# A second layer's first input: fetched through GpSimd's queue into a place of its own, split late by ScalarE

## The chip, the core and the metric

The kernel runs on one core of one Trainium2 chip. The metric is the device time of one execution in microseconds (us); lower is better. Three runs of the kernel before gave 1139.18, 1139.20 and 1141.53 us, median 1139.2 us. One core issues work to five engines: TensorE (PE in the profile; its weight loads are PEld), VectorE (DVE), ScalarE (ACT), GpSimd (POOL) and SyncE (SP). SP and POOL also issue DMAs, each in the order of its own queue.

## The reference

Three stages follow each other. A delta-rule attention (4 batches, 8 heads, 768 steps, 48 features per head) makes 3072 tokens of 384 features. Two feed-forward layers then work on these tokens:

```python
h = x @ w_in                                   # 3072 x 384 @ 384 x 2048
g = np.maximum(h, 0.0) + alpha * np.minimum(h, 0.0)
x = g @ w_out                                  # 3072 x 2048 @ 2048 x 384
h = np.maximum(x @ w2_in, 0.0)
out = h * h @ w2_out
```

## The kernel before, in words

**Precision.** Every operand of a large matmul is split into a high and a low part (`xh`, `xl`; `gh`, `gl`; `wh`, `wl`), and each product is three matmuls: high by high, high by low, low by high. The high part is a pass of ScalarE (a copy with a cast), the low part a subtraction on VectorE.

**Loops.** The first layer (layer 0) takes the tokens in 12 chunks of 256 (t = 0 to 11), the second (layer 1) in 6 chunks of 512. In each chunk, j runs over 16 slices of the 2048 hidden features. `emit_h` (line 623) makes h of slice j with 9 matmuls (L632), turns it into g and splits it: in layer 0 ScalarE's scaled copy (L110), VectorE's maximum (L639), ScalarE's `gh` (L644) and VectorE's `gl` (L645). `emit_acc` (line 648) multiplies g with the slice of the output weights in 9 matmuls (L664), three slices of j later in layer 0 and two later in layer 1, and adds them up in the accumulators in PSUM. After the last j, ScalarE copies the accumulators out (L673, tile `xf`), and SP stores them to `x2d` in DRAM (L675). The accumulators of the next chunk are the same banks, so its first L664 waits for L673 of the chunk before.

**Inputs of a chunk.** `load_x(n)` (line 551) fetches the input, `take_x(n)` (line 562) splits it. For n = 0 to 11 this is a chunk of the first layer. For n = 12 to 17 it is a chunk of the second layer, which consists of two halves of 256 tokens, each a load of 384 KB from `x2d` through SP (L560). One half goes into the tile `xf` of the pool `moe`, which has one buffer and which the first layer's inputs and outputs share; the other goes into a tile `xf` of the pool `w2`. `take_x` makes six ScalarE passes (L569) and six VectorE subtractions (L570): three blocks m of 128 features by two halves.

**Weights of the second layer.** `load_w1(j, i)` (line 723) fetches a raw block through GpSimd's queue into one of three buffers (L725) and unpacks it: a scaled copy on ScalarE (L110, `t<-raw`), four steps on VectorE (L589 to L592), an addition (L734), ScalarE's `wh` (L735), VectorE's `wl` (L736). That is 32 blocks; for each j the first (i = 0) holds the input weights, the second the output weights. The pool `w2` is opened when the attention's pools are closed, 20 steps before the end of the first layer, so this work runs beside the last two chunks of layer 0 and the first chunk of layer 1.

**What sets the order.** Work is emitted from a list of events by due time (`at`, `run_to`), in steps of one slice j of layer 0: chunk t has steps 16 t to 16 t + 15, and the second layer starts at step 192. The due time becomes a priority (`urgency`; earlier is more urgent). When the program is built, a planner simulates the engines and puts on each, whenever it is free, the most urgent instruction that is ready in the simulation. On the chip each engine then runs its instructions strictly in the order thus written down, whatever the real times are. `tc.issue_after(ins)` keeps instructions behind `ins` on the same engine. The due times around the change: `load_w1` 172 to 188.5; `load_x(12)` 187, `take_x(12)` 189; the last slices of layer 0 at 190 and 191; the first of layer 1 at 192.

**The tile `t` of pool `w`.** It has one buffer of 768 floats per partition. The attention writes its output there (line 523) before SP stores it to `x1d` (L528); after the last chunk of the attention nothing uses it.

Of the kernel before, what the change touches and what calls it, by code (L numbers as in the profile page):

```python
# [9 lines left out]
F32 = mybir.dt.float32  # L10
# [11 lines left out]
DM, DFF = 384, 2048  # L22
CH = 64
NCH = S // CH
NU = 2 * NCH
NG = 8
TOK = B * CH
KD = DM // 128
NF = DFF // 128
# [6 lines left out]
TT = -3  # L36
# [29 lines left out]
TB = 1  # L66
# [12 lines left out]
CHAIN = 4  # L79
EARLY = 3  # L80
INV = 15
WQ = 8
UR = 7
WN = 11
# [6 lines left out]
def kernel(ctx: ExitStack, tc: tile.TileContext, qT, ktok, vtok, beta, w1, w2, alpha, cmask, hmask, eye, ident, out):  # L91
    nc = tc.nc

    def pool(name, stack=ctx, **kw):
        return stack.enter_context(tc.tile_pool(name=name, bufs=1, **kw))

    e_stack, s_stack, w_stack = (ExitStack() for _ in range(3))
    const, moe, wpool = pool("const"), pool("moe"), pool("w")
# [5 lines left out]
    V, G, A = nc.vector, nc.gpsimd, nc.scalar  # L104

    def new(p, shape, dt, tag, bufs=1):
        return p.tile(shape, dt, tag=tag, name=tag, bufs=bufs)

    def scaled(out, in_, scale=1.0):
        A.activation(out=out, in_=in_, func=ACTF.Copy if isinstance(scale, float) else ACTF.Identity, scale=scale)  # L110
# [60 lines left out]
    x2d = [dram.tile([128, KD, 2, TOK], F32, tag=f"x2d{n}", name=f"x2d{n}") for n in range(NCH // 2)]  # L171
# [47 lines left out]
    def at(t, f, *a, ahead=0.0):  # L219
        heapq.heappush(events, (t, seq[0], f, a, ahead))  # L220
        seq[0] += 1
# [327 lines left out]
    xf = {}  # L549

    def load_x(n):

        if n < NCH:
            xf[n] = [new(moe, [128, KD, TOK], F32, "xf")]
            nc.sync.dma_start(out=xf[n][0][0:HD], in_=x1d[n][:, 0:KD])
            nc.sync.dma_start(out=xf[n][0][HD:128], in_=x1d[n][:, KD].rearrange("(m p) i -> p m i", m=KD))
        else:
            xf[n] = [new(moe, [128, KD, TOK], F32, "xf"), new(w2p[0], [128, KD, TOK], F32, "xf")]
            for h, t in enumerate(xf[n]):
                nc.sync.dma_start(out=t, in_=x2d[n - NCH][:, :, h])  # L560

    def take_x(n):
        src = xf.pop(n)
        p, k = (moe, XB) if n < NCH else (w2p[0], 1)
        xs[n] = [tuple(new(p, [128, len(src) * TOK], F32R, f"x{t}{m}", k) for t in "hl") for m in range(KD)]
        for m, (xh, xl) in enumerate(xs[n]):
            for h, t in enumerate(src):
                cols = slice(TOK * h, TOK * h + TOK)
                A.copy(out=xh[:, cols], in_=t[:, m])  # L569
                (G if m in TG and n < NCH else V).tensor_tensor(out=xl[:, cols], in0=t[:, m], in1=xh[:, cols].bitcast(F32), op=ALU.subtract)  # L570


# [21 lines left out]
    def load_w0(j):  # L594

        raw = new(wpool, [128, 4 * DM], F32, f"w{j}")
        if j < WQ:
            G.dma_start(out=raw.bitcast(I64), in_=w1[j])
# [19 lines left out]
            A.copy(out=wl[i], in_=ps[i])  # L618


    gt, acc = {}, {}

    def emit_h(layer, t, j):
        wh, wl = (t[0] for t in wt[layer, j])
        p, w = (w2p[0], 2 * TOK) if layer else (moe, TOK)
        ps = psum.tile([128, 512], F32, tag="h", name="h", bufs=2)[:, :w]
        n = 0
        for m in range(KD):
            sl = slice(m * 128, m * 128 + 128)
            xh, xl = xs[layer * NCH + t][m]  # L630
            for a, x in ((wh, xh), (wh, xl), (wl, xh)):
                nc.tensor.matmul(ps, lhsT=a[:, sl], rhs=x, start=(n == 0), stop=(n == 8))  # L632
                n += 1
        g = new(p, [128, w], F32, "r1", RB if layer else R1)
        if layer == 0:


            scaled(g, ps, sgn[:, j:j + 1])
            V.scalar_tensor_tensor(out=g, in0=ps, scalar=bet[:, j:j + 1], in1=g, op0=ALU.mult, op1=ALU.max)  # L639
        else:  # L640
            A.activation(out=g, in_=ps, func=ACTF.Relu)  # L641
            A.activation(out=g, in_=g, func=ACTF.Square)  # L642
        gh, gl = (new(p, [128, w], F32R, n, LAGB + 1 if layer else GB) for n in ("gh", "gl"))
        A.copy(out=gh, in_=g)  # L644
        (V if layer or j not in GP else G).tensor_tensor(out=gl, in0=g, in1=gh.bitcast(F32), op=ALU.subtract)  # L645
        gt[layer, t, j] = gh, gl

# [34 lines left out]
    for c in range(NCH):  # L682
# [17 lines left out]
        def scan(k=k, t=e0 + 9, n=IN):  # L700
            ops = inverse(k)
            for i, f in enumerate(ops):
                at(t + i * n / len(ops), f, ahead=(IA0, IA1)[k] if k < 2 else INV)
        if c % 2:
# [5 lines left out]
    for n in range(NCH + NCH // 2):  # L710
        t = 16 * n if n < NCH else 32 * n - 16 * NCH
        at(t - 5, load_x, n)
        at(t + TT, take_x, n)
    for j in range(NF):
        at(W0T + j, load_w0, j, ahead=AW)
    end = 16 * NCH
# [21 lines left out]
    w2p = []  # L738
# [7 lines left out]
    for layer, t, j in [(0, t, j) for t in range(NCH) for j in range(NF)] + [(1, t, j) for t in range(NCH // 2) for j in range(NF)]:  # L746
        step = 1 + layer
        now = 16 * NCH * layer + step * (16 * t + j)
        run_to(now)
        urgency(now - HURRY)  # L750
        emit_h(layer, t, j)
        run_to(now + 0.5 * step)
        pend.append((layer, t, j))
        urgency(now + 0.5 * step - HURRY)
        while len(pend) > (LAGB if layer else LAG):
            emit_acc(*pend.pop(0))
# [80 lines left out]
```

## Time and profile before

| | |
|---|---|
| median of three runs | 1139.2 us |
| profiled execution | 1140.61 us |
| its span | 1138.8 us |
| PE busy | 1054.2 us (93%) |
| DVE busy | 736.5 us (65%) |
| ACT busy | 728.6 us (64%) |
| mean granted clock of TensorE | 0.975 of full speed |

The span is what the trace covers; the execution has 1.8 us more around it, and it took 1.4 us more than the median of the three runs. A row of a timeline gives the start, the length, the engine, the line, the operation, what was written from what, and, in brackets, how long the engine had been idle before and what it had waited for. An engine whose queue is blocked by a wait stands still even if later work in its order is ready.

### The profile page before, as it was taken

How to read it: one execution, taken by the hardware profiler on the slowest of the kernel's cores; microseconds unless marked ns; L12 is line 12 of the kernel's file. 1: busy time of each engine (PE TensorE's matmuls, PEld its weight loads, DVE VectorE, ACT ScalarE, POOL GpSimd, SP SyncE). 2: the span in 40 equal slices, each digit the busy share in tenths (PEclk: the TensorE clock that was granted, in tenths of full speed). 3: DMA queues.
4: the chain of work that ended last, by engine and by line, in shares of the span. 5: the costliest groups of instructions: out<-in, count | busy, mean ns of one | idle time of the engine just before them, and what ended most of it. 6: DMA issues, size and time to landing. Idle time of an engine off the chain costs nothing.

```text
span 1138.8 us, 25230 instructions
## 1 busy us (share of the span) xinstructions
PE 1054.2 (93%) x9952; PEld 935.1 (82%) x9952; DVE 736.5 (65%) x1904; ACT 728.6 (64%) x1583; POOL 118.7 (10%) x206
## 2 busy tenths in 40 slices
PE   2766889899999979999999989999999999999997
PEld 2434579899999979999999989988888888888886
DVE  6998789699789869988986759888312121221211
ACT  7867678777767866885566546577645454454543
POOL 5111111111111111110110001011000000000000
PEclk9988899999999989999999989999999999999999
DMA  9585457545545464464353143343101000010000
GB/s 307 121 297 124 108 138 183 128 138 138 136 115 150 137 156 114 131 164 112 80 136 87 46 131 98 94 141 109 56 1 56 0 28 28 1 56 1 28 1 28
DMA packets 162886, 116.78 MB, mean 103 GB/s; under 512 B 122032, under 2 KB 143536, under 8 KB 162768
## 3 DMA queue, kind: packets, MB, share of 16 engines
q0 software_dynamic: 16320, 67.45, 19.3%
q1 hardware_dynamic: 146448, 47.73, 17.6%
q8 instruction: 78, 1.28, 0.5%
q14 instruction: 40, 0.33, 0.1%
HBM read 75.82 MB, written 39.32 MB: 101 GB/s over the span
## 4 chain that ended last, share of the span: by engine, by line
PE 73%; issue 8%; DMA 7%; DVE 6%; ACT 4%; SPq 1%; POOL 1%; POOLq 0%; ACTq 0%; DVEq 0%
PE h L632 32%; PE acc L664 31%; PE pa L133 3%; PE pa L123 3%; PE h L612 1%; DMA prob<-gscr 1%; DMA xf<-x2d 1%; PE h L613 1%; DMA xf<-x1d 1%; DMA al<-in_alpha_dram 1%; DMA gscr<-pf 1%; DMA vr<-in_vtok_dram 1%; ACT kbdE L110 1%; PE pe L351 0%; DVE w L590 0%
## 5 line engine op out<-in xcount | busy, mean ns | idle before, releaser
L632 PE MATMUL h<-xh,w 128*128 128x256 f32 (+1 forms) x1728 | 440.1, 325 | 4.7 <-DVE r L639 3.2
L664 PE MATMUL acc<-gh,w 128*128 128x256 f32 (+1 forms) x1728 | 431.8, 323 | 6.8 <-ACT xf L673 5.5
L632 PEld LDWEIGHTS h<-xh,w 128*128 128x128 f32 x1728 | 304.2, 192 | 29.8 <-DVE r L639 4.5
L645 DVE TENSOR_TENSOR gl<-r,gh 128x256 fp32r<-128x256 f32 (+1 forms) x288 | 145.4, 507 | 277.8 <-ACT gh L644 277.5
L664 PEld LDWEIGHTS acc<-gh,w 128*128 128x128 f32 x1728 | 299.1, 192 | 30.4 <-ACT xf L673 6.3
L632 PE MATMUL h<-xl,w 128*128 128x256 f32 (+1 forms) x864 | 278.5, 322 | 0.0
L664 PE MATMUL acc<-gl,w 128*128 128x256 f32 (+1 forms) x864 | 275.2, 322 | 3.6 <-DVE gl L645 3.4
L664 PEld LDWEIGHTS acc<-gl,w 128*128 128x128 f32 x864 | 165.2, 191 | 16.5 <-DVE gl L645 4.7
L632 PEld LDWEIGHTS h<-xl,w 128*128 128x128 f32 x864 | 166.2, 192 | 11.1
L644 ACT CAST gh<-r 128x256 fp32r<-128x256 f32 (+1 forms) x288 | 136.0, 476 | 52.9 <-DVE r L639 44.9
L641 ACT ACTIVATE r<-h 128x512 f32<-128x512 f32 x96 | 57.1, 596 | 148.0 <-PE h L632 141.2
L110 ACT ACTIVATE r<-h,sgn 128x256 f32<-128x256 f32 x192 | 89.9, 472 | 61.8 <-PE h L632 56.4
L639 DVE SCALAR_TENSOR_TENSOR r<-h,bet,r 128x256 f32<-128x256 f32 x192 | 90.9, 476 | 20.8 <-ACT r L110 19.9
L398 DVE TENSOR_TENSOR inv<-inv,col 128x252 f32<-128x252 f32 (+22 forms) x186 | 63.8, 343 | 1.7
L397 DVE TENSOR_TENSOR col<-prob,inv 128x252 f32<-128x252 f32 (+22 forms) x186 | 63.5, 341 | 1.5
L642 ACT ACTIVATE r<-r 128x512 f32<-128x512 f32 x96 | 60.7, 633 | 2.6
L123 PEld LDWEIGHTS <-kbd 96*128 96x128 f16 x1104 | 38.7, 99 | 7.7 <-issue 3.2
L612 PE MATMUL h<-w,idf 128*128 128x384 f32 x64 | 35.8, 648 | 7.3 <-ACT w L618 7.3
L133 PE MATMUL pa<-ph,ubd 128*128 128x64 f16 (+1 forms) x576 | 38.7, 194 | 0.9 <-ACT ubd L110 0.9
L569 ACT CAST xh<-xf 128x256 fp32r<-128x256 f32 x72 | 25.3, 403 | 20.0 <-DMA xf<-x2d 8.5
L570 DVE TENSOR_TENSOR xl<-xf,xh 128x256 fp32r<-128x256 f32 x72 | 26.6, 420 | 15.1 <-ACT xh L569 15.1
L133 PE MATMUL pa<-qh,sbd 96*128 96x64 f16 (+1 forms) x528 | 35.3, 194 | 0.0
(176 smaller groups left out, 1392.0 us busy)
## 6 DMA issues: line engine op xcount, KB each, us to landing
raw<-in_w_dram POOLq DMA_DIRECT2D x32, 384.0 KB, 3.4
kbd<-fscr POOLq DMA_DIRECT2D x22, 384.0 KB, 4.2
ktb<-kscr POOLq DMA_DIRECT2D x22, 384.0 KB, 3.6
kscr<-ktbE POOLq DMA_DIRECT2D x21, 384.0 KB, 3.4
fscr<-kbdE POOLq DMA_DIRECT2D x21, 384.0 KB, 3.4
w<-in_w_dram POOLq DMA_DIRECT2D x8, 768.0 KB, 9.2
w<-in_w_dram SPq DMA_DIRECT2D x8, 768.0 KB, 12.2
vr<-in_vtok_dram POOLq DMA_DIRECT2D x24, 192.0 KB, 4.1
```

Source lines behind the costliest of these rows:

```text
L110: A.activation(out=out, in_=in_, func=ACTF.Copy if isinstance(scale, float) else ACTF.Identity, scale=scale)
L123: nc.tensor.matmul(ps, lhsT=w[:, i], rhs=x[:, j], start=start and n == 0, stop=stop and n == 2)
L133: nc.tensor.matmul(ps[0:w.shape[1], g], lhsT=w, rhs=x[:, j, g], start=start and n == 0, stop=stop and n == 2)
L397: V.tensor_tensor(out=t, in0=row, in1=x[:, :, 0:m, j:j + 1].to_broadcast([128, 2, m, n]), op=ALU.mult)
L398: i = V.tensor_tensor(out=x[:, :, 0:m, j + 1:], in0=x[:, :, 0:m, j + 1:], in1=t, op=ALU.subtract)
L632: nc.tensor.matmul(ps, lhsT=a[:, sl], rhs=x, start=(n == 0), stop=(n == 8))
L639: V.scalar_tensor_tensor(out=g, in0=ps, scalar=bet[:, j:j + 1], in1=g, op0=ALU.mult, op1=ALU.max)
L641: A.activation(out=g, in_=ps, func=ACTF.Relu)
L642: A.activation(out=g, in_=g, func=ACTF.Square)
L644: A.copy(out=gh, in_=g)
L645: (V if layer or j not in GP else G).tensor_tensor(out=gl, in0=g, in1=gh.bitcast(F32), op=ALU.subtract)
L664: i = nc.tensor.matmul(acc[m], lhsT=a[:, sl], rhs=g, start=(j == 0 and n == 0 and (layer == 1 or m != 1)), stop=(j == NF - 1 and n == 2), ...
```

## The change

The second layer's first input (n = 12) is loaded by two DMAs of GpSimd's queue in place of SP's. Its first half goes into the tile `t` of pool `w` in place of the shared `xf`; the other half goes where it went. Its `take_x` is emitted at step 191.4 in place of 189, and its six ScalarE passes are kept behind `gh` of slice j = 14 (the fifteenth) of the last chunk of layer 0.

```diff
+XG = 1
...
         else:
-            xf[n] = [new(moe, [128, KD, TOK], F32, "xf"), new(w2p[0], [128, KD, TOK], F32, "xf")]
+            one = new(wpool, [128, 2 * DM], F32, "t", TB).rearrange("p (m i) -> p m i", m=KD) if n == NCH else new(moe, [128, KD, TOK], F32, "xf")
+            xf[n] = [one, new(w2p[0], [128, KD, TOK], F32, "xf")]
             for h, t in enumerate(xf[n]):
-                nc.sync.dma_start(out=t, in_=x2d[n - NCH][:, :, h])
+                (G if n == NCH and XG else nc.sync).dma_start(out=t, in_=x2d[n - NCH][:, :, h])
...
-                A.copy(out=xh[:, cols], in_=t[:, m])
+                with tc.issue_after(last[NF - 2]) if n == NCH else nullcontext():
+                    A.copy(out=xh[:, cols], in_=t[:, m])
...
-    gt, acc = {}, {}
+    gt, acc, last = {}, {}, {}
...
-        A.copy(out=gh, in_=g)
+        i = A.copy(out=gh, in_=g)
+        if (layer, t) == (0, NCH - 1):
+            last[j] = i.ins
...
-        at(t + TT, take_x, n)
+        at(t + (TT if n != NCH else -0.6), take_x, n)
```

## Rows read from the trace of the kernel before

**Rows 1.** The page: busy time by engine, and the last chain's share by line.

```profile
PE 1054.2 (93%) x9952; PEld 935.1 (82%) x9952; DVE 736.5 (65%) x1904; ACT 728.6 (64%) x1583; POOL 118.7 (10%) x206
...
PE h L632 32%; PE acc L664 31%; PE pa L133 3%; PE pa L123 3%; PE h L612 1%; DMA prob<-gscr 1%; DMA xf<-x2d 1%; PE h L613 1%; DMA xf<-x1d 1%; DMA al<-in_alpha_dram 1%; DMA gscr<-pf 1%; DMA vr<-in_vtok_dram 1%; ACT kbdE L110 1%; PE pe L351 0%; DVE w L590 0%
```

**Rows 2.** The chain followed back, 640 to 812 us: start, length, what.

```profile
662.26 6.96 DMA xf<-x2d
...
710.70 3.93 DMA xf<-x2d
...
737.99 0.24 PE acc L664 x2
...
740.29 1.91 PE acc L664 x16
```

**Rows 3.** Timeline of PE, around 667 and 716 us.

```profile
666.85 0.28 PE L664 MATMUL acc<-gh,w 128*128 128x256 f32 x1
671.02 0.58 PE L664 MATMUL acc<-gh,w 128*128 128x256 f32 x1 [3.89 <-ACT xf L673]
...
716.02 0.51 PE L664 MATMUL acc<-gh,w 128*128 128x256 f32 x2 [1.30 <-ACT gh L644]
717.04 0.39 PE L664 MATMUL acc<-gl,w 128*128 128x256 f32 x1 [0.51 <-DVE gl L645]
```

**Rows 4.** Windows: length, PE, PEld, DVE, ACT, POOL busy (count), PEclk, DMA share, GB/s.

```profile
671.02:676.73 5.71, 5.71 (x26) 5.71 (x27) 4.43 (x12) 1.93 (x5) 0.00 (x0) 0.50 0.44 142
717.04:721.27 4.23, 4.23 (x22) 4.23 (x23) 3.96 (x11) 2.20 (x6) 0.54 (x1) 0.60 0.00 2
722.00:738.00 16.00, 16.00 (x136) 16.00 (x135) 14.54 (x37) 9.07 (x22) 1.61 (x3) 1.00 0.31 94
745.00:785.00 40.00, 40.00 (x181) 33.20 (x181) 34.95 (x78) 29.21 (x57) 6.07 (x11) 1.00 0.43 129
```

**Rows 5.** Timeline of ACT, around 670 and 715 us.

```profile
669.32 1.02 ACT L569 CAST xh<-xf 128x256 fp32r<-128x256 f32 x3 [5.04 <-DMA xf<-x2d]
...
670.61 0.36 ACT L673 COPY xf<-acc 128x256 f32<-128x256 f32 x1
670.86 0.56 ACT L110 ACTIVATE t<-raw 128x384 f32<-128x384 f32 x1
...
714.65 1.02 ACT L569 CAST xh<-xf 128x256 fp32r<-128x256 f32 x3 [3.49 <-DMA xf<-x2d]
```

**Rows 6.** SP's queue, 640 to 765 us, and landing of x1d's stores.

```profile
656.39 5.33 SPq L528 DMA_DIRECT2D x1d<-t  x2
...
710.70 0.57 SPq L560 DMA_DIRECT2D xf<-x2d  x1
...
x1d<-t SPq DMA_DIRECT2D x2, 192.0 KB, 2.7
```

**Rows 7.** Line L725 (raw blocks, GpSimd's queue), 655 to 676 us.

```profile
L725 POOL DMA_DIRECT2D raw<-in_w_dram x3: 536/538/540, 661.7 to 662.7; - x3
...
DMA to landing us min/median/max: 4.7/5.4/6.5
```

**Rows 8.** Timeline of DVE: the two groups of three subtractions.

```profile
669.75 1.10 DVE L570 TENSOR_TENSOR xl<-xf,xh 128x256 fp32r<-128x256 f32 x3 [5.02 <-ACT xh L569]
...
715.09 1.10 DVE L570 TENSOR_TENSOR xl<-xf,xh 128x256 fp32r<-128x256 f32 x3 [2.91 <-ACT xh L569]
```

**Rows 9.** Timeline of ACT: `gh` of the last chunk's fifteenth slice.

```profile
736.38 0.41 ACT L644 CAST gh<-r 128x256 fp32r<-128x256 f32 x1 [0.59 <-DVE r L639]
```

**Rows 10.** Timelines of ACT and DVE: splitting the second layer's second input.

```profile
801.21 2.07 ACT L569 CAST xh<-xf 128x256 fp32r<-128x256 f32 x6 [0.81 <-PE h L632]
...
801.65 2.12 DVE L570 TENSOR_TENSOR xl<-xf,xh 128x256 fp32r<-128x256 f32 x6 [0.66 <-ACT xh L569]
```

**Rows 11.** The second layer's slice j = 15: `wh` on ACT, first matmul on PE.

```profile
796.86 0.55 ACT L735 CAST w<-raw 128x384 fp32r<-128x384 f32 x1 [0.38 <-DVE raw L734]
...
798.97 0.39 PE L632 MATMUL h<-xh,w 128*128 128x512 f32 x1
```

## The prediction

> **What bounds the kernel now.** I read the page first: TensorE is busy for 93% of the span, and the chain that ended last is mostly its matmuls L632 and L664 [rows 1]. That chain's lines also name a transfer, xf<-x2d, 1% of the span. Following the chain through 640 to 812 us shows where: twice, for 6.96 and 3.93 us, the end of the kernel hangs on a load of a second-layer input [rows 2], in the middle of the first layer. From 722 us on TensorE has no idle time in the windows read [rows 4], so a microsecond it saves before can reach the end, if nothing else comes late.
>
> What do the two loads hold up? ScalarE's timeline says it: it stands 5.04 us in front of three passes L569 and later 3.49 us in front of the other three [rows 5]. The order is fixed, so all behind them waits. At 669 us that is L673, the copy that frees an accumulator: TensorE stops for 3.89 us until L673 of 670.61 [rows 3, 5]. At 714 us it is a gh: TensorE stops for 1.30 us, then for 0.51 us on its gl [rows 3]. None of these six passes is needed before layer 1 begins at 738 us.
>
> **The two stalls, in TensorE's time.** Undisturbed, 136 matmuls take 16.00 us, 0.118 us each, at a granted clock of 1.00 [rows 4]. After the first stop 26 matmuls took 5.71 us at 0.50 (the 1.2 GHz level), which is 5.71 - 26 x 0.118 = 2.6 us too many; after the second 22 took 4.23 us, 1.6 us too many [rows 4]. So the first stall costs 3.89 + 2.6 = 6.5 us, the second 1.30 + 0.51 + 1.6 = 3.4 us, together 9.9 us.
>
> **What the change removes.** The passes go behind the fifteenth slice's gh, which begins at 736.38 us [rows 9], so neither stop can be caused by them. On the TensorE side that is worth up to 9.9 us. SP's queue loses both loads; the second of them could only be issued at 710.70 us, because it used the shared tile [rows 6]. The second half's tile is now freed late, so SP's load of the second layer's second input into that tile moves behind the passes, to about 740 us; its reader is at 801.21 us [rows 10], so that costs nothing, and it would cost only if it landed some 60 us late.
>
> **What it adds.** (a) Two DMA issues on GpSimd, about 0.54 us each as the raw blocks have [rows 7], on an engine busy for 1.61 of 16 us [rows 4]; the data is wanted 70 us later. Nothing is lost if they stand behind the three raw loads that start at 661.7 us. If they stand ahead, those wait until the last x1d store has left tile t: its issue ends at 661.7 us (656.39 + 5.33), it lands about 2.7 us after its issue [rows 6]. They then also share the transfer with two more blocks. The raw landings of 4.7, 5.4 and 6.5 us after issues 0.5 us apart [rows 7] put one block at about 1.4 us. That is 2.3 + 2 x 1.4 = 5 us later at worst, nothing or a small gain at best; I take nothing, since the raw loads are due long before (172 against 187).
>
> In the rows the first raw block landed 4.7 us after its issue with SP's load beside it [rows 7]. The Trainium skill, DMA: Bandwidth & Descriptors, section "Queues, rings and completion order", says that a DMA engine takes turns between queues and works through one queue in order. By that the x loads, moved into the raw blocks' queue, hold back none that stands ahead of them, and the first block could even land some 0.5 us sooner; every block behind them waits for both. The sum stays as it is; no run here shows it yet.
>
> (b) Six passes and six subtractions directly before layer 1's first h. At the next chunk boundary the same twelve took 801.21 to 803.77 us, 2.6 us [rows 10]. From the end of gh at 736.8 us that is 739.4 us. Before, 18 matmuls of L664 stood after the last h of layer 0 [rows 2]; 2.1 us of them can stand ahead of the waiting h, from 738.0 to 740.1 us. So the loss is 0 at one end. At the other end no L664 covers and VectorE, busy for 14.54 of 16 us [rows 4], is slow: 739.4 - 738.0 plus about 1 us, some 2.4 us. I take 0.5 us.
>
> **What is late next: the weights of layer 1.** The stream of blocks runs mostly on VectorE, beside the end of layer 0 and the first chunk of layer 1, and its last slice comes just in time: wh of j = 15 is ready at 796.86 + 0.55 = 797.41 us, its first matmul starts at 798.97 us [rows 11]: 1.6 us of slack. TensorE can gain 9.9 us only if this stream gains 8.3. Its start: the first t<-raw ran at 670.86 us, behind the stopped passes [rows 5], while its block had landed at 661.7 + 4.7 = 666.4 us [rows 7]: 4.4 us to gain. In the second stop VectorE stood for 2.91 us [rows 8], which it gains. The first three subtractions (1.0 us) ran before the stream and now run inside it: 1.0 us lost; the other three were inside already. Sum 4.4 + 2.9 - 1.0 = 6.3, with the slack 7.9 us.
>
> **Sum.** The smaller of 9.9 - 0.5 and 7.9 is 7.9 us. TensorE then waits some 1.5 us before j = 15, close to the 1.81 us after which the clock fell and cost 1.6 us. I take half, 0.8: the gain is 7.1 us, and 1140.6 becomes 1133.5 us for an execution like the profiled one. Against the median (1.4 us less) it is 1132.1 us.
>
> **Rivals.**
> Free: weights come in time after all and all 9.9 us count, less 0 to 0.8: 1129.3 to 1130.1 us. For it: without the stops VectorE may fill its gaps better (5 of 40 us in 745 to 785 [rows 4]). Against: the 1.6 us of slack. Chance 0.14.
>
> The stream does not start earlier: the x loads ahead of the raw blocks (5 us, above), or ScalarE waiting for a raw block in front of L673, which leaves part of the first stop. Then the weights gain 0 + 2.9 - 1.0 + 1.6 = 3.5 us: 1135.7 us. In favour: the blocks landed between 666.4 and 669.2 us, while L673 is wanted at 667. Against: the planner had put L673 before t<-raw [rows 5]. Chance 0.18.
>
> Nothing measurable: that rival, and the boundary takes 2.4 us more: gain 1.1, 1138.1 us. A change without its effect belongs here too: the planner orders the rest anew, and ScalarE stands at another wait for as long. Chance 0.07.
>
> Slower: the six subtractions (2.1 us) have a later due time than all the weight work, and VectorE's idle share is only 1.46 of 16 us [rows 4]. If they get that share alone, they take 2.1 / 0.091 = 23 us. The 18 matmuls cover 2.1 us, TensorE stops 21 us and loses 2.6 us more at the low clock: 23.6 - 9.9 = 13.7 us slower, 1152.9 us. It decides from some 9.6 us of stop on (9.6 + 2.6 - 9.9 = 2.3). Against: a stopped TensorE leaves VectorE without layer 0's work, so the share grows. Chance 0.06.
>
> **Numbers.** My forecast, 1132.1 us, has the remaining 0.55, from 1130.5 us (no clock loss) to 1134.5 us (boundary at its upper end). 0.2%, about what a measurement of this kernel can tell from no change, is 2.3 us. Faster by more: 0.55 + 0.14 + 0.18 = 0.87; within: 0.07; slower: 0.06. The range takes in the free case and the late stream with about 0.5 us: 1129.2 to 1136.2 us; outside lie the last two cases and the edges.
>
> **What would show it.** Right: no ACT wait on xf<-x2d before 736 us, no PE gap on L673 near 667, a granted clock of 1.00 from 664 to 722, t<-raw near 666.5, layer 1's first 512-column matmul near 728 to 729, its six passes just before, and a PE gap of 1 to 2 us before j = 15, near 790 us, with its wh some 6 us earlier than the 797.41 us of now. Wrong: a gap at the boundary over 3 us; a raw landing after 669 us; a PE gap at L673 that stays; or no gap at all near 790, which makes the free case true.

## The result, and the profile after

The changed kernel took 1132.13 us (median of 13 runs, 1129.48 to 1136.72), the kernel before on the same chips 1143.12 us (13 runs, 1139.18 to 1148.42). The ratio is 0.9906, 95% interval 0.9884 to 0.9928: faster by 10.7 us, between 8.2 and 13.3 (the medians alone differ by 11.0 us). The forecast time of 1132.1 us agrees better than its reasons deserve. It set a gain of 7.1 us off against 1139.2 us, the median of three runs, and both the gain and the kernel before came out larger.

The profiled execution after the change took 1134.28 us, its span 1132.5 us. Lines have moved by a few: L569 is L572 (passes), L570 is L573 (subtractions), L632 is L635, L664 is L669, L673 is L678, L725 is L730, L735 is L740, L639 is L642.

The page, against [rows 1]: the transfer xf<-x2d is gone from the last chain.

```profile
PE 1053.3 (93%) x9952; PEld 933.1 (82%) x9952; DVE 736.5 (65%) x1904; ACT 727.8 (64%) x1583; POOL 121.0 (11%) x208
...
PE h L635 30%; PE acc L669 30%; PE pa L134 3%; PE pa L124 2%; ACT kbdE L111 1%; DMA prob<-gscr 1%; PE h L615 1%; DMA gscr<-pf 1%; PE h L616 1%; DMA vr<-in_vtok_dram 1%; DMA al<-in_alpha_dram 1%; ACT kf L111 1%; ACT r L111 0%; DVE gl L650 0%; ACT w L621 0%
```

The timeline of TensorE after, against [rows 3]. Of the 3.89 us in front of the accumulators 0.73 are left; the stops of 1.30 and 0.51 us have no successor. One chunk later TensorE waits 0.35 us for the same kind of copy. Layer 1 begins at 732.20 us.

```profile
671.54 0.38 PE L669 MATMUL acc<-gh,w 128*128 128x256 f32 x1 [0.73 <-ACT xf L678]
...
703.31 0.39 PE L669 MATMUL acc<-gh,w 128*128 128x256 f32 x1 [0.35 <-ACT xf L678]
...
732.20 0.40 PE L635 MATMUL h<-xh,w 128*128 128x512 f32 x1
...
792.28 0.39 PE L635 MATMUL h<-xh,w 128*128 128x512 f32 x1
```

Windows after, against [rows 4] (length, PE, PEld, DVE, ACT, POOL, PEclk, DMA share, GB/s): the clock stays at 1.00 right behind the 0.73 us, and from 714 us on TensorE has no listed idle time.

```profile
671.54:676.00 4.46, 4.46 (x37) 4.46 (x38) 4.46 (x13) 2.88 (x7) 0.00 (x0) 1.00 0.64 222
...
714.00:732.00 18.00, 18.00 (x153) 18.00 (x152) 17.38 (x46) 11.34 (x29) 2.56 (x5) 1.00 0.36 103
...
740.00:800.00 60.00, 60.00 (x270) 49.78 (x269) 51.17 (x113) 41.99 (x83) 8.00 (x14) 1.00 0.38 114
```

ScalarE and GpSimd after, against [rows 5, 7, 9]. ScalarE still stands in front of the accumulator copy L678, 2.35 us, now for the first raw weight block. The six passes run without a wait from 730.51 us. GpSimd issues the two x loads behind three raw blocks.

```profile
670.32 0.54 ACT L111 ACTIVATE t<-raw 128x384 f32<-128x384 f32 x1 [2.35 <-DMA raw<-in_w_dram]
...
671.13 0.36 ACT L678 COPY xf<-acc 128x256 f32<-128x256 f32 x1
...
730.51 0.41 ACT L572 CAST xh<-t 128x256 fp32r<-128x256 f32 x1
...
789.96 0.53 ACT L740 CAST w<-raw 128x384 fp32r<-128x384 f32 x1
```

```profile
665.38 1.60 POOL L730 DMA_DIRECT2D raw<-in_w_dram  x3 [33.99 <-PE acc L669]
666.97 0.77 POOL L562 DMA_DIRECT2D xf<-x2d  x1
668.08 0.76 POOL L562 DMA_DIRECT2D t<-x2d  x1 [0.34 <-issue]
```

**A measure that leaves the noise out.** The two programs have the same instructions in the same order up to the place of the first pass on each engine; only SP's first load is missing. Yet the first raw block of layer 1's weights was issued at 661.7 us before ([rows 7]) and at 665.4 us after. What the change does lies behind this issue. So I use the *stretch*, from this issue to the end of the span: 1138.8 - 661.68 = 477.1 us before, 1132.5 - 665.38 = 467.1 us after. The change takes 10.0 us out of it in this pair of profiles, each of which is one execution.

### The profile page after: what moved, and what is told of

Read it like the earlier page. It is cut to its first block, busy times and chain, and to the rows that moved or that the text cites. A ratio compares the mean times of both kernels' runs of the same rounds, so it can differ in the third digit from the quotient of the medians.

```text
span 1132.5 us, 25229 instructions
## 1 busy us (share of the span) xinstructions
PE 1053.3 (93%) x9952; PEld 933.1 (82%) x9952; DVE 736.5 (65%) x1904; ACT 727.8 (64%) x1583; POOL 121.0 (11%) x208
## 4 chain that ended last, share of the span: by engine, by line
PE 69%; issue 10%; DMA 7%; ACT 7%; DVE 6%; POOL 1%; SPq 1%; POOLq 0%; DVEq 0%; ACTq 0%
PE h L635 30%; PE acc L669 30%; PE pa L134 3%; PE pa L124 2%; ACT kbdE L111 1%; DMA prob<-gscr 1%; PE h L615 1%; DMA gscr<-pf 1%; PE h L616 1%; DMA vr<-in_vtok_dram 1%; DMA al<-in_alpha_dram 1%; ACT kf L111 1%; ACT r L111 0%; DVE gl L650 0%; ACT w L621 0%
## 5 line engine op out<-in xcount | busy, mean ns | idle before, releaser
L635 PE MATMUL h<-xh,w 128*128 128x256 f32 (+1 forms) x1728 | 438.4, 324 | 4.2 <-DVE r L642 2.6
L669 PE MATMUL acc<-gh,w 128*128 128x256 f32 (+1 forms) x1728 | 429.7, 321 | 2.1 <-ACT xf L678 2.0
L635 PEld LDWEIGHTS h<-xh,w 128*128 128x128 f32 x1728 | 302.9, 192 | 29.2 <-DVE r L642 3.5
L669 PEld LDWEIGHTS acc<-gh,w 128*128 128x128 f32 x1728 | 297.6, 190 | 25.7 <-ACT xf L678 2.8
L669 PE MATMUL acc<-gl,w 128*128 128x256 f32 (+1 forms) x864 | 274.5, 322 | 4.6 <-DVE gl L650 4.5
L635 PE MATMUL h<-xl,w 128*128 128x256 f32 (+1 forms) x864 | 277.6, 322 | 0.0
L669 PEld LDWEIGHTS acc<-gl,w 128*128 128x128 f32 x864 | 164.4, 190 | 17.3 <-DVE gl L650 5.6
L635 PEld LDWEIGHTS h<-xl,w 128*128 128x128 f32 x864 | 165.6, 192 | 11.1
L642 DVE SCALAR_TENSOR_TENSOR r<-h,bet,r 128x256 f32<-128x256 f32 x192 | 90.9, 476 | 16.4 <-ACT r L111 15.1
L134 PEld LDWEIGHTS <-ubd 128*128 128x128 f16 (+1 forms) x576 | 31.1, 100 | 2.1 <-ACT ubd L111 1.2
L124 PE MATMUL pa<-qh,kbd 96*128 96x64 f16 x576 | 30.3, 196 | 2.7 <-DVE uh L120 1.0
```

Of the source, the lines that this page charges most:

```text
L124: nc.tensor.matmul(ps, lhsT=w[:, i], rhs=x[:, j], start=start and n == 0, stop=stop and n == 2)
L134: nc.tensor.matmul(ps[0:w.shape[1], g], lhsT=w, rhs=x[:, j, g], start=start and n == 0, stop=stop and n == 2)
L669: i = nc.tensor.matmul(acc[m], lhsT=a[:, sl], rhs=g, start=(j == 0 and n == 0 and (layer == 1 or m != 1)), stop=(j == NF - 1 and n == 2), ...
```

## The experiments

All numbers of the traces in one table (us). "First t<-raw" and "wh 15" (ScalarE's pass for slice 15's input weights of layer 1) are counted from the first raw block's issue; "VectorE idle" is VectorE's idle time from the first unpacking step to wh 15. Each row is one profile. A "ratio" below is that of timed runs to the kernel before: e1, e3 and e6 were timed in 10 to 12 executions, the other experiments rest on their one profiled execution.

| kernel | span | raw issue | stretch | first t<-raw | wh 15 | VectorE idle |
|---|---|---|---|---|---|---|
| before | 1138.8 | 661.68 | 477.1 | 9.2 | 135.2 | 15.0 |
| before, again (e11) | 1142.0 | 663.74 | 478.3 | 9.8 | 136.9 | 16.3 |
| change | 1132.5 | 665.38 | 467.1 | 4.9 | 124.6 | 8.2 |
| change, again (e10) | 1138.7 | 671.30 | 467.4 | 5.0 | 124.6 | 7.6 |
| e1 passes late only | 1134.6 | 667.68 | 466.9 | 5.0 | 123.5 | 7.7 |
| e2 loads only | 1131.3 | 663.23 | 468.1 | 4.5 | 125.1 | 8.7 |
| e3 loads on SP | 1135.5 | 668.42 | 467.1 | 4.7 | 123.5 | 8.1 |
| e4 first stop removed | 1137.8 | 667.14 | 470.7 | 5.0 | 129.4 | 12.5 |
| e5 second stop removed | 1134.8 | 661.47 | 473.3 | 9.4 | 132.2 | 12.6 |
| e6 copy first | 1132.5 | 665.36 | 467.1 | 4.7 | 123.8 | 7.8 |
| e7 16 more copies | 1139.3 | 665.08 | 474.2 | 4.9 | 135.6 | 12.8 |
| e8 32 more copies | 1144.3 | 668.77 | 475.5 | 4.7 | 136.4 | 10.7 |
| e9 passes behind slice 15 | 1139.3 | 669.95 | 469.4 | 5.0 | 125.1 | 8.4 |

### How well the stretch repeats (e10, e11)

Both kernels unchanged, profiled once more.

> The changed kernel once more, for how well the stretch repeats: 467.1 us within 0.3 us, while the time ahead of the first raw block's issue (665.4 us in the profile shown) may differ by some us. If the stretch is off by over 1 us, the differences of 1 us between the other kernels say nothing.

> The kernel before once more: stretch 477.1 us within 0.5 us (it holds two stops on transfers), both stops at the same matmuls and as long within 0.5 us.

The change repeats within 0.3 us. The kernel before comes out 1.1 us longer, more than the half microsecond expected, because its stops are longer by 0.6 and 0.8 us: here TensorE's timeline of e11, where [rows 3] had 3.89 and 1.30 us.

```profile
673.70 0.58 PE L664 MATMUL acc<-gh,w 128*128 128x256 f32 x1 [4.52 <-ACT xf L673]
...
719.31 0.50 PE L664 MATMUL acc<-gh,w 128*128 128x256 f32 x2 [2.12 <-ACT gh L644]
```

From this one repeat of each I take a profile of the changed kernel as good to some 0.3 us and one of the kernel before to about 1 us; the second pair gives 478.3 - 467.4 = 10.9 us. The two pairs bracket the 10.7 us of the timed runs. Some 0.4 us of either difference lies behind the last store and has nothing to do with the stops; e3 shows it.

### Passes late, loads as before (e1)

```diff
-                A.copy(out=xh[:, cols], in_=t[:, m])
+                with tc.issue_after(last[NF - 2]) if n == NCH else nullcontext():
+                    A.copy(out=xh[:, cols], in_=t[:, m])
...
-        at(t + TT, take_x, n)
+        at(t + (TT if n != NCH else -0.6), take_x, n)
```

> Loads as before (SP's queue, one half in the shared tile), only the six ScalarE passes late. Measure: the stretch from the first raw block's issue to the end of the span, 477.1 us before and 467.1 us after the change; the work ahead of it is the same list of instructions. Theory A (the place of the passes in ScalarE's queue is all): both stops go, 466.2 to 467.6 us, ratio to before 0.990 to 0.993. Rival B (the loads' own place and queue bring the gain): at least 3.4 us of it is missing, 470 us or more.

Stretch 466.9 us, ratio 0.9919 (0.9893 to 0.9945): the late passes alone bring all of it. TensorE (length, PE, PEclk, DMA share, GB/s) has no gap at all in the first 20 us:

```profile
667.68:687.68 20.00, 20.00 (x169) 1.00 0.59 177
```

Rival B falls as far as it says that the loads are needed.

### Loads as in the change, passes early (e2)

```diff
-                with tc.issue_after(last[NF - 2]) if n == NCH else nullcontext():
+                with nullcontext():
...
-        at(t + (TT if n != NCH else -0.6), take_x, n)
+        at(t + TT, take_x, n)
```

> Loads as in the change (GpSimd's queue, own place), passes due as early as before and free to stand anywhere. Theory A: ScalarE comes to the passes near 672 us while the loads, issued at 667 and 668 us behind three raw blocks, land some 4 to 6 us later; it stands 1 to 3 us, TensorE stops behind it for up to 2 us: stretch 468 to 471 us. Rival B: the loads alone bring the whole gain, 467 us, with no wait of ScalarE on them.

Stretch 468.1 us: 9.0 of the 10.0 us come from the loads alone too. ScalarE does wait for one of them, 1.30 us, and TensorE stops for 0.28 and 0.89 us, without a lower clock. First ScalarE, then TensorE of e2, last its window behind the 0.89 us, with the columns of [rows 4]:

```profile
671.32 1.02 ACT L572 CAST xh<-xf 128x256 fp32r<-128x256 f32 x3 [1.30 <-DMA xf<-x2d]
673.38 1.00 ACT L572 CAST xh<-t 128x256 fp32r<-128x256 f32 x3
```

```profile
668.95 0.38 PE L669 MATMUL acc<-gh,w 128*128 128x256 f32 x1 [0.28 <-ACT xf L678]
...
677.89 0.39 PE L635 MATMUL h<-xh,w 128*128 128x256 f32 x1 [0.89 <-DVE r L642]
```

```profile
677.89:681.89 4.00, 4.00 (x33) 4.00 (x34) 3.41 (x9) 1.59 (x4) 0.55 (x1) 1.00 0.81 250
```

In e2 the planner puts the passes a few places later in ScalarE's order, behind the accumulator copy and one more slice, and the second half no longer waits for the shared tile. The two halves of the change are two cures for one thing; together they bring hardly more than either. The figures that theory A gave for this run came out, at their lower edge; as the statement that the late passes are what counts it is too narrow.

### The loads on SP's queue (e3)

```diff
-XG = 1
+XG = 0
```

> The change with its two loads on SP's queue instead of GpSimd's. Theory A: the queue is worth nothing, stretch 466.2 to 467.6 us. Rival C (GpSimd's queue spares something, because SP's loads stand beside the raw blocks or SP's queue is blocked by them): the first raw blocks land over 1 us later than after the change and the stretch is 1 us longer or more, over 468 us.

Stretch 467.1 us, ratio 0.9923 (0.9897 to 0.9949), the first t<-raw 4.7 us after the raw issue against 4.9: for the time of the whole the queue is worth nothing here. The prediction had weighed the Trainium skill's DMA: Bandwidth & Descriptors, "Queues, rings and completion order", for a first block some 0.5 us sooner behind a shared queue, a figure for which it gave no working. In the chain after the change the first block took 4.71 us from its issue, the same 4.7 us as with SP's load beside it [rows 7], so the runs do not show that half microsecond; that the loads stood behind the blocks and held none of the first three back agrees. The slowest of the first three blocks did land sooner, 5.6 us after its issue against 7.0 in e3, so that part of rival C is right; the stretch was no shorter for it. The first block's transfer after the change, and the landings of the first three blocks after the change and in e3:

```profile
665.38 4.71 DMA raw<-in_w_dram
...
DMA to landing us min/median/max: 4.7/5.2/5.6
...
DMA to landing us min/median/max: 4.5/5.3/7.0
```

Nothing in sum is not nothing in each part. In e3 the planner left the accumulator copy ahead of the first t<-raw, the gap of 0.73 us is absent, and ScalarE's last copy of the kernel begins 0.4 us sooner, at 463.1 us of the stretch against 463.5. But from the issue of the last store to the end of the span e3 takes 3.3 us and the change 3.0. The last store of the change, then of e3:

```profile
1129.49 0.33 SPq L674 DMA_DIRECT2D out_dram<-r  x1
...
1132.15 0.33 SPq L674 DMA_DIRECT2D out_dram<-r  x1
```

At the end SyncE waits for its transfers one by one, and the order of these waits differs: after the last store has landed, seven more of them (some 0.06 us each) follow in e3 and one after the change. The profiles divide by the queue: 3.3 us in the kernel before, its repeat, e1, e3, e4 and e5, and 3.0 us in the change, its repeat, e2 and e6 to e9.

### One stop at a time (e4, e5)

Kernel before with a `last` as in the change; in e4 only the half in pool `w2` (h = 1), in e5 only the half in the shared tile (h = 0) is kept late:

```diff
-                A.copy(out=xh[:, cols], in_=t[:, m])
+                with tc.issue_after(last[NF - 4]) if n == NCH and h == 1 else nullcontext():
+                    A.copy(out=xh[:, cols], in_=t[:, m])
```

> Kernel before, only the three passes of the half in pool w2 (the first stop, 5.04 us) kept behind gh of slice j = 12 of the last chunk; loads and the other three passes as before. Stretch from the first raw block's issue to the end: 477.1 us before. Theory A (the stops add up, 6.5 and 3.4 us, and the stream of weights follows TensorE): 470.2 to 471.0 us, the second stop as before. Rival D (the stream of weights gains only its earlier start, 4.4 us, less three subtractions, 1.0 us, and has 1.6 us of slack, as the prediction's sum had it): TensorE stops before slice 15 of layer 1, 472.1 us or more.

> Kernel before, only the three passes of the half in the shared tile (the second stop, 3.49 us) kept behind gh of slice j = 12 of the last chunk. Theory A: the first stop as before (about 3.9 us and the low clock after it), the second gone, 473.4 to 474.1 us. Rival E (the second stop hides behind the first: with it gone TensorE meets the stream of weights sooner): 475 us or more, with a gap before a slice of layer 1.

Stretches 470.7 and 473.3 us: 6.5 and 3.8 us gained, where the prediction had 6.5 and 3.4 (against the longer second profile of the kernel before, 1.1 us more each). TensorE's timeline of e4, then of e5, shows that in each the other stop stays:

```profile
716.70 0.50 PE L668 MATMUL acc<-gh,w 128*128 128x256 f32 x2 [0.96 <-ACT gh L646]
717.73 0.39 PE L668 MATMUL acc<-gl,w 128*128 128x256 f32 x1 [0.53 <-DVE gl L649]
```

```profile
670.98 0.58 PE L668 MATMUL acc<-gh,w 128*128 128x256 f32 x1 [4.07 <-ACT xf L677]
```

Together 10.3 us, so the stops add up, as far as one profile each can tell. Rival D's gap before slice 15 in e4 did not come.

### The last small gap (e6)

```diff
-        scaled(t, high.bitcast(F32), 2.0 ** -112)
+        with tc.issue_after(last["o"]) if (j, i) == (0, 0) else nullcontext():
+            scaled(t, high.bitcast(F32), 2.0 ** -112)
```

where `last["o"]` is chunk 9's second accumulator copy (m = 1), the one TensorE waited for.

> The change, and the first unpacking pass of layer 1's weights (t<-raw) kept behind the accumulator copy that TensorE waited 0.73 us for at 671 us. Theory A: that gap goes and nothing else moves, stretch 466.2 to 466.6 us against 467.1. Rival: the stream of weights starts no earlier and the gap turns into another wait, 467 us or more.

The gap of 0.73 us is gone, and the stretch is 467.1 us as before it; ratio 0.9926 (0.9902 to 0.9951). The rival is right. The 0.7 us reappear in pieces too short for the timeline's brackets, just before the next chunk of layer 0: in 12 us there TensorE began 90 matmuls in e6, and 97 in the same 12 us after the change, at the same clock. Seven matmuls at 0.118 us are 0.8 us. What held them up in e6 was not tried. The window of e6, then of the change, with the columns of [rows 4]:

```profile
693.36:705.36 12.00, 11.83 (x90) 10.90 (x89) 12.00 (x32) 8.62 (x23) 1.11 (x2) 1.00 0.32 100
...
693.38:705.38 12.00, 11.65 (x97) 11.40 (x96) 11.83 (x31) 8.73 (x24) 1.49 (x3) 1.00 0.27 87
```

e1 and e3 have no gap of 0.73 us either and end within 0.2 us of the change; they are ahead of it at the last copy, by 0.6 and 0.4 us, and lose most of that in the longer end described at e3.

### More work in the stream of weights (e7, e8)

```diff
         V.tensor_tensor(out=f, in0=high.bitcast(F32), in1=f, op=ALU.add)
+        if 2 * j + i < 16:
+            V.tensor_copy(out=f, in_=f)
```

(e8: 32 in place of 16.) The copies are needless work and change no value.

> The change, and one needless VectorE copy of 128x384 in each of the first 16 of the 32 weight blocks of layer 1, about 0.3 us each, some 5 us in all. Rival D (the stream is VectorE's alone and has 1.8 us of slack before slice 15): TensorE stops for 3 us, stretch 470 us or more against 467.1. Theory A (the stream has idle VectorE time ahead of it, 9 of 60 us from 740 to 800, and catches up): 467.0 to 468.0 us, no gap of 1 us before a slice of layer 1.

> The same needless copy in all 32 blocks, some 10 us in all, more than VectorE's idle time in the stretch. Rival D: 475 us or more. Theory A: part is taken from idle time, part not: 468 to 472 us, with TensorE's gaps in the last slices of layer 1's first chunk.

Stretches 474.2 and 475.5 us. In e7 VectorE's busy time from the first unpacking step to wh 15 rose from 110.9 to 117.4 us, 6.5 us, and the stretch by 7.1 us: the stream did not catch up, as rival D said. The time is lost at the last slices of layer 1's first chunk, by the pattern this case began with: ScalarE stands for a transfer, a gh behind it is late, TensorE stops. The transfer itself was issued late, after GpSimd had stood 4.30 us for VectorE. GpSimd, ScalarE, then TensorE of e7:

```profile
791.20 0.54 POOL L730 DMA_DIRECT2D raw<-in_w_dram  x1 [4.30 <-DVE raw L592]
...
794.84 0.56 ACT L111 ACTIVATE t<-raw 128x384 f32<-128x384 f32 x1 [1.99 <-DMA raw<-in_w_dram]
...
798.29 0.62 ACT L647 CAST gh<-r 128x512 fp32r<-128x512 f32 x1
```

```profile
798.97 0.97 PE L669 MATMUL acc<-gh,w 128*128 128x512 f32 x3 [3.21 <-ACT gh L647]
```

All stops of that chunk in e7 add up to 4.9 us. Behind the longest the granted clock was 0.67 from 800 to 805 us, in which TensorE began 15 matmuls where the next 5 us had 24; that is some 1.6 us more. The two make 6.5 of the 7.1 us. The windows, with the columns of [rows 4]:

```profile
800.00:805.00 5.00, 4.73 (x15) 3.84 (x16) 3.28 (x8) 2.09 (x5) 0.00 (x0) 0.67 0.00 0
805.00:810.00 5.00, 5.00 (x24) 4.00 (x23) 2.27 (x6) 3.78 (x9) 0.00 (x0) 1.00 0.47 140
```

e8 doubled the copies and lost only 1.3 us more; rival D's 475 us holds for it, but the loss is not in proportion.

### The passes four microseconds later (e9)

```diff
-                with tc.issue_after(last[NF - 2]) if n == NCH else nullcontext():
+                with tc.issue_after(last[NF - 1]) if n == NCH else nullcontext():
```

> The change, with the six passes kept behind the gh of the last slice (j = 15) of layer 0 instead of j = 14, about 2 us later. Theory A (18 to 27 matmuls L669 of the last slices cover them, the sum's 0 to 2.4 us at the boundary): a gap of at most 1 us before layer 1's first h, stretch from the first raw block's issue to the end 467.0 to 468.5 us against 467.1. Rival F (the boundary was as tight as it could be): a gap of 1.5 us or more with a low clock behind it, 469 us or more.

Stretch 469.4 us, 2.0 to 2.2 us over the change. The passes begin 69.2 us after the raw issue (739.10 - 669.95) instead of 65.1 (730.51 - 665.38). No single gap there is long, and the clock stays at 1.00: at the boundary TensorE's timeline of e9 lists 0.16, 0.27 and 0.24 us, 0.7 us in all.

```profile
739.91 0.70 PE L635 MATMUL h<-xh,w 128*128 128x512 f32 x2 [0.16 <-ACT xh L572]
741.36 0.38 PE L669 MATMUL acc<-gh,w 128*128 128x256 f32 x1 [0.27 <-ACT xf L678]
...
745.88 0.50 PE L635 MATMUL h<-xh,w 128*128 128x512 f32 x1 [0.24 <-ACT r L644]
```

Between the two theories: the loss is that of rival F, its form is not, and two thirds of it stand in no listed gap. The boundary has room for the passes behind j = 14 and no longer for the same passes behind j = 15.

## Why the prediction was right, and where it was not

**The stops: right.** Two stops at ScalarE's passes, worth 6.5 and 3.4 us: removed singly they gave 6.5 and 3.8 us, together 10.0 and 10.9 us in the two pairs, of which 0.4 us belong to the end of the kernel (e3). That end the prediction had at nothing when it took both loads off SP's queue. The clock's share was read rightly: TensorE at 1.00 where it had 0.50 and 0.60 [rows 4].

**What was to be late next: mis-sized.** The step of the prediction that failed is in the sum: "The smaller of 9.9 - 0.5 and 7.9 is 7.9 us", with a wait of 1.5 us before j = 15 and 0.8 us for a lower clock. The start of the stream of weights gained 4.2 us (9.18 to 4.94), against 4.4 worked out. But its wh 15 came 10.6 us earlier (135.18 to 124.58), against 6.3: behind the start the stream got 6.3 us shorter (125.41 to 119.07) where the sum had 2.9 - 1.0 = 1.9. So TensorE's first matmul of slice 15, at 792.28 us, still had 1.8 us of slack behind the pass that ended at 790.49 (789.96 + 0.53), where it had 1.6 [rows 11]. No gap came, and neither did the 0.8 us.

I had treated the stream as VectorE's work with one idle time, the 2.91 us of [rows 8]. VectorE's windows from the first unpacking step to wh 15, before and after, show more: 125.41 - 110.39 = 15.0 us idle before, 119.07 - 110.89 = 8.2 us after. The part up to layer 1's first matmul stands under each: 66.61 - 58.49 = 8.1 us idle before, 61.31 - 58.89 = 2.4 us after. So 5.7 of the 6.8 us come from layer 0.

```profile
671.45:796.86 125.41, 122.95 (x768) 112.62 (x768) 110.39 (x263) 79.51 (x173) 15.74 (x29) 0.97 0.38 114
671.45:738.06 66.61, 64.15 (x497) 63.49 (x497) 58.49 (x148) 37.35 (x92) 6.98 (x13) 0.93 0.36 108
```

```profile
670.89:789.96 119.07, 118.07 (x764) 108.28 (x765) 110.89 (x267) 79.93 (x176) 16.35 (x29) 1.00 0.41 124
670.89:732.20 61.31, 60.31 (x499) 60.01 (x499) 58.89 (x150) 39.28 (x98) 7.81 (x14) 1.00 0.40 122
```

VectorE's waits in these windows, before and then after (who waited for what: us in total, times, longest):

```profile
DVE r L639 <- ACT r L110: 4.8, 11, 1.7
DVE raw L589 <- ACT t L110: 4.2, 8, 1.3
DVE xl L570 <- ACT xh L569: 2.9, 1, 2.9
DVE w L736 <- ACT w L735: 1.9, 3, 1.1
```

```profile
DVE raw L592 <- ACT t L111: 8.8, 12, 2.5
DVE gl L650 <- ACT gh L647: 0.4, 1, 0.4
DVE r L642 <- ACT r L111: 0.2, 1, 0.2
```

Before, VectorE stood 4.8 us in front of layer 0's maximum L639, with unpacking steps behind it in its order; after, 0.2 us. The stream shares VectorE's order with work that follows TensorE, so it does not run at a pace of its own. The table fits this: with one stop left (e4, e5) VectorE's idle time is 12.5 and 12.6 us, with none (change, e1, e3, e6) 7.7 to 8.2, and wh 15 moves with the stretch. How much of this is TensorE's stops and how much the new order that the planner wrote was not separated, so this cause is argued and not shown.

Whether the slack was read rightly stays open. With 1.8 us of it, e7's 6.5 us of added work should show as 4.7 us of stops, and 4.9 were there; in e8 VectorE was busy for 9.5 us more up to wh 15, which should show as 7.7 us, and the stops in layer 1's first chunk were 5.6 us. The stream has little room, though it did not bound this gain; a further gain of TensorE's was not tried.

**The boundary: right in kind.** The prediction took 0.5 us between 0 and 2.4. After the change TensorE lists no gap there; e9 put 2.0 to 2.2 us on the upper end.

**Rivals.** The free case, 9.9 us, given 0.14, is nearest to what happened, and the prediction's own sign for it, no gap near 790 us, is what the trace shows. Its reason was wrong in part: it expected VectorE to fill gaps of layer 1, and most of the time came from layer 0. The case of a late stream had one true part: ScalarE does wait for a raw block in front of the accumulator copy (2.35 us), because with the loads on GpSimd's queue the planner turned the order of [rows 5] round; TensorE stops for 0.73 us only. The slower case did not occur: VectorE made all six subtractions in one run from 732.35 us, right behind the passes. The case without effect fell.

**The level.** 1132.1 us was worked out from a kernel before of 1139.2 us. Over 13 runs that kernel has 1143.1 us, 3.9 us more, and the gain was 10.7 instead of 7.1, 3.6 us more. The two errors cancel; that the forecast met the measured time is luck.

No kernel of this study beats the change: e1, e3 and e6 end within 0.3 us of it in the stretch, and their ratios lie inside each other's intervals.

## What to carry to other kernels

Where each engine keeps a written order, look for an early instruction that waits for a transfer and that nobody needs yet: the price is paid by what stands behind it, here a copy and a gh that TensorE wanted, plus the low clock after the stop. To move it behind its transfer, or to give the transfer a place and queue where it need not wait, is the same cure; either brought 9 to 10 us here. When asking what will be late next, do not take a stream of work on a shared engine as rigid: list what that engine waits for along the whole stream: waits on the work that is being sped up may shrink with it, as VectorE's 15.0 us did here to 8.2.

## What the runs showed that was not expected

The part ahead of the first raw block's issue has the same instructions in the same order on TensorE, VectorE and ScalarE in all these kernels, and it took from 661.5 (e5) to 671.3 us (e10), a spread as large as the gain. TensorE's granted clock differs there from execution to execution; the windows from 100 to 200 us, before and after the change, show 0.93 and 0.88 (length, PE, PEclk, DMA share, GB/s).

```profile
100.00:200.00 100.00, 84.62 (x1072) 0.93 0.60 144
```

```profile
100.00:200.00 100.00, 84.82 (x1033) 0.88 0.56 132
```

Whether the clock makes the whole spread was not tried. The three runs first shown for the kernel before lay at the low end of it.

Some short gaps left the clock alone: after 0.73 us (change), 0.89 us (e2) and 1.06 us (e8, 791.20 to 795.20 us) the windows show 1.00, while the 1.30 and 0.51 us of the kernel before were followed by 0.60 [rows 3, 4]. The length of a gap does not settle it: 0.96 and 0.53 us in e4 were followed by 0.60 too (717.73 to 722.00 us).

SyncE's order of waits at the very end, 3.3 or 3.0 us, was not thought of: two loads more or fewer on its queue, over 400 us earlier, changed it (e3).
